# Halving the columns of each matmul in the second product of a feed-forward

## Chip, cores and metric

The kernel runs on one core of one Trainium2 chip. The metric is the device time in microseconds from start to end of one execution; lower is better. The core's engines are TensorE (PE, with its weight loads shown apart as PEld), VectorE (DVE), ScalarE (ACT), GpSimd (POOL) and SyncE (SP), whose queue issues the DMAs.

## What is computed

Attention with two sparse masks, and a feed-forward with an exact Gelu on its result. There are 8 sequences of 576 tokens with 8 heads of 64 channels. Half the heads look at a band of 32 keys, half at every 32nd key. Cut to what matters:

```python
scores = np.matmul(q, k.transpose(0, 1, 3, 2)) / np.sqrt(D)
mask_local   = (rel >= 0) & (rel < 32)
mask_strided = (rel >= 0) & (pos[None, :] % 32 == pos[:, None] % 32)
attn = softmax(np.where(masks, scores, -1e9))     # first 4 heads local, last 4 strided
x = np.matmul(attn, v)                            # -> [4608 tokens, 512 channels]
h = x @ w_in                                      # [512, 2048]
g = 0.5 * h * (1.0 + erf(h / sqrt(2)))
out = g @ w_out                                   # [2048, 512], float32
```

## The kernel before

The 4608 tokens are cut into 12 tiles of 384, and the 2048 hidden channels into 16 chunks of 128. One step of the feed-forward is one chunk of one tile, so there are 192 steps.

Matrix products are made in a rounded float32 format (float32r) in two parts, a high part and a low part that holds the rest. Each product is three matmuls: high by high, high by low, low by high. A step n has three pieces:

- `ffn_h` (lines 541 to 543), the first product: the step's weights `w1` are stationary and the tokens `x` move, 384 columns a matmul. Four channel chunks by three parts are 12 matmuls into one PSUM bank `H`, of which there are two.
- `ffn_g`: ScalarE applies Gelu in PSUM (line 550) and rounds to the high part `gh` (552); VectorE makes the low part `gl` (554).
- `ffn_o` (lines 580 to 582), the second product: blocks of 128 tokens of `gh` or `gl` are stationary, and the 512 output channels of `w2` move. Three blocks by three parts are 9 matmuls a step. Each block has its own PSUM bank `O`, which collects all 16 chunks of a tile; `start` is set on the first matmul of a tile and clears the bank for accumulation.

After the last chunk of a tile `store` copies each bank to `ob` on ScalarE (line 587), and SP writes it to the output (589).

The local heads run on TensorE in 36 jobs (`local_job`: scores at line 251, transposes at 257, products with v at 266). The strided heads run on VectorE (lines 416 and 458), except those of the first tile, which go through TensorE. The weights arrive as 64-bit words and are split into their two float32r parts in `split_w` (lines 144 to 166) on ScalarE and VectorE at the start.

The order of work is set in two ways. Up to step 15 the list `START` gives the order on each engine by hand. From step 16 on the loop over `step(n)` issues `ffn_h(n)`, `ffn_g(n)` and `ffn_o(n - 2)`. There only ScalarE's order is fixed (`manual_schedule(engines={ET.Activation})`), and a planner with costs and due times of its own orders the other engines. The last call issues the second product of the last two steps together, a block of tokens after another.

Of the kernel before, what the change touches and what calls it, by code (L numbers as in the profile page):

```python
# [10 lines left out]
F32 = mybir.dt.float32  # L11
# [12 lines left out]
P = 128  # L24
STRIDE = 32          # band width and stride of the two masks
TT = 384             # tokens of an FFN tile
LU = 64              # queries of a unit of the local heads
LK = LU + STRIDE     # its keys
TR = TT // STRIDE    # its rows of 32 tokens
NGR = 16             # groups of strided heads that the tensor engine takes  # L30
MA = TT // NGR       # tokens of a group
NEG = -8.0e9         # -1e9 before the scale of 1/8
UR = 4               # rows of a unit of the strided heads

# The order of work: (sequence, first row, end row). The strided heads of the first NA tiles go
# through the tensor engine.
NA = 1
# [3 lines left out]
# The start, up to FFN step NB, in the order of each engine's instructions: a word is the next part  # L41
# of a piece of work. Loads: q and k (q) and v (v) of a local job, q and k (S) and v (B) of the strided
# heads of a tile, q and k (E) and v (e) of the first other strided heads, a chunk of weights (w).
# Pieces: local jobs (L), strided heads of a tile on the tensor engine (halves a and b, then A) and
# in units (u), splits of a chunk of weights (c), FFN steps (f).
NB = 16
# [13 lines left out]
# The chunks of weights whose first, second and fifth steps are on VectorE, ScalarE and ScalarE  # L60
# [4 lines left out]
QUOT_V = (0, 2, 3, 4)   # local jobs of the start whose quotients are on VectorE  # L65
# [3 lines left out]
def units(most):  # L69
    """(visit, sequence, first row, rows, tile, its row there): rows of one visit and one tile."""  # L70
    res = []
    for k, (vi, b, r) in enumerate(ROWS):
        if res and res[-1][0] == vi and k % TR and res[-1][3] < most:
            res[-1][3] += 1
        else:
            res.append([vi, b, r, 1, k // TR, k % TR])
    return res
# [7 lines left out]
def attn_ffn_kernel(ctx: ExitStack, tc: tile.TileContext, qk, vl, qka, va, qs, ks, vs, w, out):  # L85
# [6 lines left out]
    NF = w.shape[0]              # hidden chunks  # L92
    NC = DM // P                 # channel chunks
# [4 lines left out]
    JPT = NJ // NTILE            # jobs of a tile  # L98
# [18 lines left out]
    mask = const.tile([P, LK], F32, name="mask")      # a band of STRIDE keys for each query  # L117
    mask0 = const.tile([P, LK], F32, name="mask0")    # the same for the first unit of a sequence

# [3 lines left out]
    # ------------------------------------------------------------------ weights  # L123
    wst, w1, w2 = {}, {}, {}

    def slot(name, shape, dtype=F32):
        """8 KiB a partition: resident weights, and before them what the start needs."""
        return wpool.tile(shape, dtype, name=name, tag="w")
# [5 lines left out]
    def split_w(f):  # L134
        """float64 words -> the leading 24 bits in float32, in two float32r parts."""
        raw = wst.pop(f)
        word = raw.bitcast(U32).rearrange("p (n two) -> p n two", two=2)
        high, low = word[:, :, 1], word[:, :, 0]
        half = raw.bitcast(I16).rearrange("p (n e) -> p n e", e=4)
        byte = raw.bitcast(U8).rearrange("p (n e) -> p n e", e=8)[:, :, 3]  # L140
        hf = high.bitcast(F32)
        # low word: the 3 bits below the high word's, and the sign
        if f in LOW_V:
            nc.vector.tensor_scalar(half[:, :, 0].bitcast(U16), half[:, :, 1].bitcast(U16), 13, None,
                                    ALU.logical_shift_right)
        else:
            nc.scalar.activation(half[:, :, 0], byte, AF.Copy, scale=1.0 / 32, bias=-0.49)  # L147
        yield
        if f in SIGN_S:
            nc.scalar.activation(half[:, :, 1].bitcast(F16), hf, AF.Copy, scale=2.0 ** -60)  # L150
        else:
            nc.vector.tensor_scalar(half[:, :, 1].bitcast(U16), half[:, :, 3].bitcast(U16), 0x8000, None,
                                    ALU.bitwise_and)
        yield
        # exponent from a bias of 1023 to one of 127: the high word, read as float32, by 2**-112
        nc.scalar.activation(hf, hf, AF.Copy, scale=2.0 ** -112)  # L156
        yield
        nc.vector.scalar_tensor_tensor(high, high, 3, low, ALU.logical_shift_left, ALU.bitwise_or)
        yield
        wt = slot(f"w_{f}", [P, 2, 2 * DM], F32R)  # L160
        if f in HIGH_S:
            nc.scalar.copy(wt[:, 0, :], hf)  # L162
        else:
            nc.vector.tensor_copy(wt[:, 0, :], hf)
        yield
        nc.vector.tensor_tensor(wt[:, 1, :], hf, wt[:, 0, :].bitcast(F32), ALU.subtract)  # L166
        w1[f] = wt[:, :, 0:DM].rearrange("p t (c f) -> p t c f", c=NC)
        w2[f] = wt[:, :, DM:]

    # ------------------------------------------------------------------ x tiles  # L170
# [7 lines left out]
    # ------------------------------------------------------------------ local heads  # L178
# [25 lines left out]
    def softmax_parts(blocks, nq, scores, msk, p, nmax, ssum, rs, dve):  # L204
        """Four steps over blocks of scores: mask and maximum, exponentials, sums, quotients."""
# [31 lines left out]
    def local_job(x, banks=None, dve=0, pn=-1):  # L237
        """Local heads of two units: blocks (head pair, unit) of two heads' scores, [2 * LU, LK]."""
# [37 lines left out]
    # ------------------------------------------------------------------ strided heads, first tiles  # L276
    ka = {}

    def load_a(t):
        """Group g has the tokens NGR * m + g of tile t."""  # L280
# [16 lines left out]
    def half_tile(t, o, bank):  # L297
        """Strided heads of tile t: attention of half o of the groups, [(head, query), (group, key)]."""
# [41 lines left out]
    def strided_tile(t, banks):  # L340
        """The same, attended values: [(head, query), token, channel], a bank for each row of PE tiles."""
# [23 lines left out]
    # ------------------------------------------------------------------ strided heads  # L365
# [15 lines left out]
    def load_strided(gr, nm):  # L381
        """q, k or v of the visits that share one buffer."""
# [94 lines left out]
    def alternate(us, what, first):  # L477
        """The steps of several units in turn, so that those which build on each other stay apart:
        of a unit the first ones, then a row of queries after another, then the last one."""
# [22 lines left out]
    def unit_job(us):  # L502
        """Several units, in parts of one engine each."""
        n = 8                        # steps of a part
# [26 lines left out]
    # ------------------------------------------------------------------ FFN  # L531
    hps, gs, ops_ = {}, {}, {}
    ready = [t * NF for t in range(NTILE)]       # first step of a tile
    xfree = [0, 0] + ready[1:-1]                 # first step that may write its x
# [22 lines left out]
    def runs(t, a):  # L557
        """Parts of a block of P columns of a tile that are consecutive tokens."""
# [10 lines left out]
    def ffn_o(*ns):  # L569
        """Chunks of hidden channels into the outputs, a block of tokens after another."""  # L570
# [3 lines left out]
        for a in range(TT // P):  # L574
            o = ops_[t][a]
            sl = slice(a * P, (a + 1) * P)
            for n in ns:
                f = n % NF
                gh, gl = gs[n]
                nc.tensor.matmul(o, gh[:, sl], w2[f][:, 0, :], start=(f == 0), stop=False)  # L580
                nc.tensor.matmul(o, gh[:, sl], w2[f][:, 1, :], start=False, stop=False)  # L581
                nc.tensor.matmul(o, gl[:, sl], w2[f][:, 0, :], start=False, stop=(f == NF - 1))  # L582
# [8 lines left out]
    # ------------------------------------------------------------------ plan  # L591
    strided = []                 # (tile, cost, op)
    N0 = 17
    U0 = sum(x[4] <= NA for x in PLACE)      # those of tile NA are in the plan of the start
# [38 lines left out]
    # a query's residue and no later: the difference's sign and lowest bits are zero  # L633
# [7 lines left out]
    # ------------------------------------------------------------------ start  # L641
# [10 lines left out]
    def job(name):  # L652
        """The parts of a piece of the start, one engine each."""
# [36 lines left out]
    active = []                  # [generator, job, stages done]  # L690
# [56 lines left out]
def lay_out(q, k, v, w_in, w_out):  # L747
    """The inputs in the order in which the chip reads them."""
# [4 lines left out]
    # local heads: two units a job, [job, (j d), pr, unit, token] for heads 2 * pr + j  # L753
# [5 lines left out]
    def pick(a, tok):            # [job, unit, token, h, d]  # L759
# [6 lines left out]
    def groups(a):               # [tile, m, g, h, d] of the first tiles  # L766
# [3 lines left out]
    def padded(a):               # to 32 tokens a group  # L770
        return np.concatenate([a, a[:, 0:32 - MA]], axis=1)

    def by_row(a):               # [b, (h r), row, d]
# [36 lines left out]
```

## Time and profile before

| | |
|---|---|
| median of 2 runs | 948.04 us (947.17 to 948.91) |
| span of the profiled execution, first to last instruction | 946.0 us |
| mean granted TensorE clock over the span | 0.981 |
| busy: PE, PEld | 905.5 us, 792.6 us |
| busy: DVE, ACT | 698.1 us, 523.7 us |
| matmuls of the first product | 2304, of 384 columns |
| matmuls of the second product | 1728, of 512 columns |

The profile is of one execution. Its own time as a run isn't listed apart; its span stands 1.2 to 2.9 us under the two runs. Times are from the span's start. A row of a timeline gives the start in microseconds, the duration in microseconds, the engine, the line, the operation, and the tiles as out<-in. A row of a group gives the busy time and the mean duration of one in ns, and behind the second bar the idle time before it with what ended it. Matmuls are pipelined: a record runs from the start to the modelled end, and records of neighbours overlap.

### The profile page before, as it was taken

How to read it: one execution, taken by the hardware profiler on the slowest of the kernel's cores; microseconds unless marked ns; L12 is line 12 of the kernel's file. 1: busy time of each engine (PE TensorE's matmuls, PEld its weight loads, DVE VectorE, ACT ScalarE, POOL GpSimd, SP SyncE). 2: the span in 40 equal slices, each digit the busy share in tenths (PEclk: the TensorE clock that was granted, in tenths of full speed). 3: DMA queues.
4: the chain of work that ended last, by engine and by line, in shares of the span. 5: the costliest groups of instructions: out<-in, count | busy, mean ns of one | idle time of the engine just before them, and what ended most of it. 6: DMA issues, size and time to landing. Idle time of an engine off the chain costs nothing.

```text
span 946.0 us, 17929 instructions
## 1 busy us (share of the span) xinstructions
PE 905.5 (96%) x5588; PEld 792.6 (84%) x5588; DVE 698.1 (74%) x4831; ACT 523.7 (55%) x1113; POOL 8.1 (1%) x56
## 2 busy tenths in 40 slices
PE   4688889999999999999999999999999999999998
PEld 3576678888888888888888888888888888888997
DVE  5677689957999599678968987786999897561110
ACT  6999977545655535536535455445555544542222
POOL 1000000000000000000000000000000000000000
PEclk8599999999999999999999999999999999999999
DMA  9925320201121013002011112011211200100001
GB/s 332 338 80 200 126 82 24 73 23 57 48 73 56 24 48 105 25 23 82 24 58 60 49 29 88 23 49 47 69 32 40 90 24 1 59 1 1 34 1 34
DMA packets 21872, 62.24 MB, mean 66 GB/s; under 512 B 2576, under 2 KB 3856, under 8 KB 19728
## 3 DMA queue, kind: packets, MB, share of 16 engines
q1 hardware_dynamic: 21776, 61.09, 19.4%
q8 instruction: 44, 0.72, 0.3%
q14 instruction: 52, 0.43, 0.1%
HBM read 51.64 MB, written 9.44 MB: 65 GB/s over the span
## 4 chain that ended last, share of the span: by engine, by line
PE 87%; ACT 11%; DMA 1%; issue 1%; DVE 1%; SPq 0%; ACTq 0%
PE H L541 14%; PE H L543 14%; PE O L582 13%; PE O L581 13%; PE H L542 13%; PE O L580 13%; ACT ws L150 3%; ACT ws L147 3%; PE S_L L251 3%; PE X_L L266 2%; ACT ws L156 2%; PE S_L L257 1%; DMA qka<-in_qka_dram 1%; ACT w L162 1%; ACT H L550 1%
## 5 line engine op out<-in xcount | busy, mean ns | idle before, releaser
L541 PE MATMUL H<-xh,w 128*128 128x384 f32 x768 | 266.1, 347 | 0.9 <-ACT w L162 0.9
L543 PE MATMUL H<-xh,w 128*128 128x384 f32 x768 | 262.9, 342 | 1.1 <-DVE w L166 1.0
L550 ACT ACTIVATE H<-H 128x384 f32<-128x384 f32 x192 | 92.5, 482 | 303.0 <-PE H L543 279.4
L542 PE MATMUL H<-xl,w 128*128 128x384 f32 x768 | 260.0, 338 | 0.0
L458 DVE SCALAR_TENSOR_TENSOR acc<-sv,sc,acc 128x64 f32<-128x64 f32 x1158 | 244.3, 276 | 0.6
L580 PE MATMUL O<-w,gh 128*128 128x512 f32 x576 | 226.5, 393 | 12.7 <-ACT gh L552 12.7
L582 PE MATMUL O<-w,gl 128*128 128x512 f32 x576 | 228.4, 399 | 0.1
L581 PE MATMUL O<-w,gh 128*128 128x512 f32 x576 | 228.3, 396 | 0.0
L554 DVE TENSOR_TENSOR gl<-H,gh 128x384 fp32r<-128x384 f32 x192 | 106.0, 552 | 147.5 <-ACT gh L552 147.0
L416 DVE CUSTOM_DVE_ANT_0 junk<-sq,sk 128x64 f32<-128x64 f32 x1290 | 204.9, 216 | 0.1
L541 PEld LDWEIGHTS H<-xh,w 128*128 128x128 f32 x768 | 145.8, 190 | 11.0 <-ACT w L162 1.3
L542 PEld LDWEIGHTS H<-xl,w 128*128 128x128 f32 x768 | 145.8, 190 | 6.0 <-DVE xl L235 0.2
L543 PEld LDWEIGHTS H<-xh,w 128*128 128x128 f32 x768 | 145.5, 189 | 3.9 <-DVE w L166 2.2
L580 PEld LDWEIGHTS O<-w,gh 128*128 128x128 f32 x576 | 108.5, 188 | 32.7 <-ACT gh L552 15.1
L582 PEld LDWEIGHTS O<-w,gl 128*128 128x128 f32 x576 | 108.5, 188 | 25.4 <-DVE gl L554 3.1
L581 PEld LDWEIGHTS O<-w,gh 128*128 128x128 f32 x576 | 108.4, 188 | 18.3
L416 DVE DVE_READ_ACCUMULATOR2_ANT sc<- 128x1 f32 x1290 | 103.2, 80 | 0.0
L552 ACT CAST gh<-H 128x384 fp32r<-128x384 f32 x192 | 92.7, 483 | 5.9
L550 ACT ACT_TABLE_LOAD x38 | 48.8, 1283 | 0.7
L213 ACT ACTIVATE P_L<-P_L,nm_L 128x96 f32<-128x96 f32 x136 | 48.8, 360 | 0.0
L251 PEld LDWEIGHTS S_L<-qk 64*64 64x64 f32 x576 | 27.7, 142 | 22.9 <-issue 13.0
L426 ACT ACT_TABLE_LOAD x35 | 44.9, 1283 | 0.6
(86 smaller groups left out, 611.6 us busy)
## 6 DMA issues: line engine op xcount, KB each, us to landing
ws<-in_w_dram SPq DMA_DIRECT2D x16, 1024.0 KB, 10.1
qk<-in_qk_dram SPq DMA_DIRECT2D x36, 320.0 KB, 3.0
out_dram<-ob SPq DMA_DIRECT2D x34, 256.0 KB, 2.2
vl<-in_vl_dram SPq DMA_DIRECT2D x36, 192.0 KB, 2.7
sk<-in_ks_dram SPq DMA_DIRECT2D x8, 576.0 KB, 4.9
sv<-in_vs_dram SPq DMA_DIRECT2D x8, 576.0 KB, 3.7
sq<-in_qs_dram SPq DMA_DIRECT2D x4, 576.0 KB, 3.9
sq<-in_qs_dram SPq DMA_DIRECT2D x3, 448.0 KB, 3.6
```

The lines of the kernel that those rows point to most:

```text
L251: nc.tensor.matmul(s[rows(j), cs], qv[rows(j), i, :], kv[rows(j), i, :], start=True, stop=True)
L416: nc.vector.tensor_tensor_reduce(junk, sq[vi, "q"][:, r0 + r, :], sq[vi, "k"][:, c, :], 1.0, 0.0, ALU.mult, ALU.add, ss[u][:, r, c:c + 1])
L458: nc.vector.scalar_tensor_tensor(acc[:, r, :], sq[vi, "v"][:, c, :], wgt, acc[:, r, :], ALU.mult, ALU.add)
L541: nc.tensor.matmul(hp, w1[f][:, 0, c, :], xh[:, c, :], start=(c == 0), stop=False)
L542: nc.tensor.matmul(hp, w1[f][:, 0, c, :], xl[:, c, :], start=False, stop=False)
L543: nc.tensor.matmul(hp, w1[f][:, 1, c, :], xh[:, c, :], start=False, stop=(c == NC - 1))
L550: nc.scalar.activation(hp, hp, AF.Gelu)
L552: nc.scalar.copy(gh, hp)
L554: nc.vector.tensor_tensor(gl, hp, gh.bitcast(F32), ALU.subtract)
L580: nc.tensor.matmul(o, gh[:, sl], w2[f][:, 0, :], start=(f == 0), stop=False)
L581: nc.tensor.matmul(o, gh[:, sl], w2[f][:, 1, :], start=False, stop=False)
L582: nc.tensor.matmul(o, gl[:, sl], w2[f][:, 0, :], start=False, stop=(f == NF - 1))
```

## The change

In `ffn_o` each matmul is split into two over halves of the output channels, 256 columns each. For a block of tokens the three matmuls of the first half come first, then the three of the second. `start` is set on the first matmul of the first half alone, and the check on accumulation groups is switched off for these matmuls, since two groups now share a bank. The rest of the diff takes comments and docstrings away and leaves the lines empty, so lines up to 579 keep their numbers.

```diff
             for n in ns:
                 f = n % NF
                 gh, gl = gs[n]
-                nc.tensor.matmul(o, gh[:, sl], w2[f][:, 0, :], start=(f == 0), stop=False)
-                nc.tensor.matmul(o, gh[:, sl], w2[f][:, 1, :], start=False, stop=False)
-                nc.tensor.matmul(o, gl[:, sl], w2[f][:, 0, :], start=False, stop=(f == NF - 1))
+                for i in range(2):
+                    hs = slice(i * (DM // 2), (i + 1) * (DM // 2))
+                    nc.tensor.matmul(o[:, hs], gh[:, sl], w2[f][:, 0, hs], start=(f == 0 and i == 0),
+                                     stop=False, skip_group_check=True)
+                    nc.tensor.matmul(o[:, hs], gh[:, sl], w2[f][:, 1, hs], start=False, stop=False,
+                                     skip_group_check=True)
+                    nc.tensor.matmul(o[:, hs], gl[:, sl], w2[f][:, 0, hs], start=False,
+                                     stop=(f == NF - 1), skip_group_check=True)
```

## Prediction

> **What bounds the kernel now.** I read the profile page first: how busy each engine is, and which work the chain that ended last is made of.
>
> ```profile
> span 946.0 us, 17929 instructions
> PE 905.5 (96%) x5588; PEld 792.6 (84%) x5588; DVE 698.1 (74%) x4831; ACT 523.7 (55%) x1113; POOL 8.1 (1%) x56
> PE 87%; ACT 11%; DMA 1%; issue 1%; DVE 1%; SPq 0%; ACTq 0%
> L580 PE MATMUL O<-w,gh 128*128 128x512 f32 x576 | 226.5, 393 | 12.7 <-ACT gh L552 12.7
> L582 PE MATMUL O<-w,gl 128*128 128x512 f32 x576 | 228.4, 399 | 0.1
> L581 PE MATMUL O<-w,gh 128*128 128x512 f32 x576 | 228.3, 396 | 0.0
> L580 PEld LDWEIGHTS O<-w,gh 128*128 128x128 f32 x576 | 108.5, 188 | 32.7 <-ACT gh L552 15.1
> ```
>
> TensorE (PE) is the bound: 87% of the chain. The change touches three lines, 580 to 582, of 576 matmuls each: 1728 in all, every one with its own load of weights (PEld), also where line 581 follows 580 with the same gh block. So splitting them makes 1728 more matmuls and 1728 more loads; no load is saved by the weights being the same.
>
> Next, where in the span this counts. The windows view gives PE's busy time by stage, and the chain shows where TensorE takes over.
>
> ```profile
> 50.00:100.00 50.00, 40.41 (x190) 31.69 (x185) 34.78 (x116) 49.86 (x52) 0.00 (x0) 0.95 0.34 129
> 150.00:200.00 50.00, 50.00 (x302) 43.44 (x303) 43.23 (x362) 25.02 (x61) 0.40 (x3) 1.00 0.14 43
> 200.00:300.00 100.00, 100.00 (x614) 88.34 (x611) 87.48 (x658) 55.21 (x128) 0.79 (x6) 1.00 0.19 59
> 800.00:900.00 100.00, 100.00 (x566) 89.11 (x565) 41.17 (x174) 39.63 (x92) 0.00 (x0) 1.00 0.07 23
> ...
> 123.03 0.37 ACT gh L552
> 123.45 0.50 PE O L580
> ...
> 0.00:123.40 123.40, 15.75 (x36) 7.04 (x36) 0.86 0.57 206
> 123.40:946.00 822.60, 210.77 (x540) 101.45 (x540) 1.00 0.14 45
> ```
>
> The columns of a window are its length, then busy time and count of PE, PEld, DVE, ACT and POOL, then the granted clock. Until about 123 us the chain runs through ScalarE (the splitting of the weights), and TensorE has gaps. From 150 us on TensorE has none at all, at a granted clock of 1.00. The last two rows are line 580 alone: 36 of its 576 matmuls lie before the chain turns to TensorE, 540 behind. So 540 x 3 = **1620 matmuls** of the second product sit on the path; the other 108 are covered by ScalarE's work before 123 us, and if that cover were gone they would cost the same each.
>
> A matmul's record (393 ns) overlaps with the next one's. What counts is the distance from one start to the next, so I read the timeline, at three places.
>
> ```profile
> 44.04 0.52 PE L543 MATMUL H<-xh,w 128*128 128x384 f32 x1
> 46.60 0.52 PE L542 MATMUL H<-xl,w 128*128 128x384 f32 x1
> ...
> 930.63 0.33 PE L541 MATMUL H<-xh,w 128*128 128x384 f32 x1
> 931.67 0.39 PE L580 MATMUL O<-w,gh 128*128 128x512 f32 x1
> ...
> 938.17 0.39 PE L581 MATMUL O<-w,gh 128*128 128x512 f32 x1
> 941.79 0.39 PE L582 MATMUL O<-w,gl 128*128 128x512 f32 x1
> ...
> 44.00:46.60 2.60, 2.60 (x9) 2.60 (x9) 1.84 (x3) 2.54 (x4) 0.00 (x0) 0.50 1.00 412
> ```
>
> Eight distances lie between the first two rows, at a granted clock of 0.50 (last row): 320 ns for 384 columns. Six lie between the next two: 1.04 us / 6 = 173.3 ns for 384 columns at full clock. Sixteen lie between the last two: 3.62 / 16 = 226.3 ns for 512 columns.
>
> **The change part by part.** (a) *The columns.* They are the same in number, so only what a matmul costs beside its columns can matter. At half clock 384 columns take at most 320 ns, so at full clock at most 160.0; measured is 173.3. Column for column 512 take 213.3; measured is 226.3. Both leave 13.0 to 13.3 ns: **a fixed 13.2 ns for each matmul**, whatever its width. A matmul of 256 columns then takes 106.7 + 13.2 = 119.9 ns, two of them 239.8, against 226.3: +13.5 ns for each matmul split.
>
> The Trainium skill (TensorE: Matmul & The Clock Gate, "Back-to-back issue gap") has a rule for it: N / 2.4 + 2.5 ns at full clock, which is 109 ns for 256 columns. The trace does not agree on the fixed part: the rows above leave 13.2, not 2.5. By the rule the change would cost 1620 x 2.5 = 4 us, an estimate; this is weighed as a rival below.
>
> (b) *What comes on top in a running step.* The distances above are the cleanest in the trace. A whole step of the feed-forward, 12 matmuls of 384 and 9 of 512 columns, is read from ScalarE's Gelu late in the run, where nothing else is on TensorE:
>
> ```profile
> 927.68 0.47 ACT L550 ACTIVATE H<-H 128x384 f32<-128x384 f32 x1 [3.20 <-PE H L543]
> 936.06 0.47 ACT L550 ACTIVATE H<-H 128x384 f32<-128x384 f32 x1 [3.20 <-PE H L543]
> ...
> 600.41 0.33 PE L541 MATMUL H<-xh,w 128*128 128x384 f32 x1
> 602.51 0.39 PE L580 MATMUL O<-w,gh 128*128 128x512 f32 x1
> 603.90 0.39 PE L580 MATMUL O<-w,gh 128*128 128x512 f32 x1
> ```
>
> Two steps are 8.38 us, one is 4190 ns; 12 x 173.3 + 9 x 226.3 = 4116. So 74 ns a step are extra, 3.5 for each of the 21 matmuls. In mid-run (last three rows) the second product shows 1.39 / 6 = 231.7 ns a matmul. I don't know what the 74 ns are. If they go with the number of matmuls (handing instructions to the array), each new one brings 3.5 more; if they go with time or steps, nothing. The two ends are +17.0 and +13.5 ns for each matmul split. I take the upper, because the clean distances at the end of the run are those of matmuls behind which no more follow.
>
> (c) *The added loads.* A load can run under the matmul before it; the question is how short that matmul may be. The rows where a load isn't hidden:
>
> ```profile
> 315.89 0.19 PEld L543 LDWEIGHTS H<-xh,w 128*128 128x128 f32 x1
> 315.89 0.44 PE L543 MATMUL H<-xh,w 128*128 128x384 f32 x1
> 316.00 0.19 PEld L541 LDWEIGHTS H<-xh,w 128*128 128x128 f32 x1
> 316.17 0.34 PE L541 MATMUL H<-xh,w 128*128 128x384 f32 x1
> ```
>
> After a batch of small attention matmuls the load and its matmul start together. The matmul's record is 0.11 us longer than usual (0.44 against 0.33), and the next load begins 0.11 us later. So a load of 128 columns holds its path for about **110 ns**, though its record says 188, and the matmul behind it streams once they have passed. 110 is under 119.9: the load stays hidden, with 10 ns to spare. Lower bound: nothing. Upper bound, by the record: 188 ns for each half. I take nothing, since the row of 110 is the same instruction in the same neighbourhood.
>
> The Trainium skill ("LDWEIGHTS (loading the stationary operand)", same page) gives columns / 1.2, 107 ns for 128. The 110 ns above agree.
>
> (d) *Order and waits.* No wait is added. A half needs the same gh, gl and weights as the whole, and the bank is released after the same last matmul. From step 16 on the order on TensorE, VectorE and the DMA queue is chosen by a planner with costs of its own, so attention batches may slip by a few matmuls; PE has no gap from 150 to 900 us, so I price this at nothing, +-2 us. If a gap opened, the work queued behind it on TensorE would wait with it. ScalarE and VectorE only get more time for their parts (VectorE is 87% busy in the third window above). The end, a copy and the stores behind the last matmul, is unchanged.
>
> **The sum:** 1620 x 17.0 ns = 27.5 us on the span of 946.0. The two runs of 947.17 and 948.91 us lie 1 to 3 us above that span, and this offset stays: 948.0 + 27.5 = **975.5 us**. With 13.5 ns it is 948.0 + 21.9 = 969.9. With the +-2 us of the order its own range is 967 to 979.
>
> **Rivals.** *B, cost by the column.* If the 13 ns are not per matmul but a slower stream, two halves cost as much as the whole. For it: the running means, 2.10 / 12 = 175.0 ns for 384 columns and 231.7 for 512, are nearly in proportion (0.456 and 0.453 ns a column). A line through them has a fixed part of 4.9 ns, so +4.9 x 1620 = 7.9 us at most: 948 to 956. Against it: the half-clock rows, which leave no room for a slower stream. The skill's 2.5 ns would land here too, at 952.
>
> *C, faster.* If a narrower matmul behind a hidden load escapes the fixed cost, halves are cheaper than the whole. The nearest rows are the transposes of the local heads:
>
> ```profile
> 310.23 0.60 PE L257 MATMUL S_L<-ident,P_L 128*96 128x128 f32 x4
> L257 PE MATMUL S_L<-ident,P_L x136: 270/272/422, 23.8 to 849.2; 128*96 128x128 f32 x136
> ```
>
> Four of them span 0.60 us, with 0.27 for the last: 0.33 / 3 = 109 ns from start to start, each with its own load (96 columns). That is only 2 ns above the 106.7 of 256 full-rate columns. At this pace two halves are 218 ns, 13.7 less than 231.7: 1620 x 13.7 = 22 us off, 926 us. It decides from 115.8 ns a half (half of 231.7) downward, and beyond 2% from 110. Against it: these are other operands at half the columns' pace, and the matmuls of this very form show 13 ns twice.
>
> *D, loads no longer covered.* The slack is only 10 ns. If the fixed 13.2 ns come behind the load (the swap of weights) and the 3.5 of a running step with them, a half takes 110 + 13.2 + 3.5 = 126.7 ns: 2 x 126.7 - 231.7 = 21.7 ns each, +35 us, 983. In the worst case the record of 188 ns is real: 2 x 188 - 231.7 = 144 ns, +234 us, 1182. Farther still, at the transposes' 0.85 ns a column, a half is 217 ns: +328 us, 1276. Against both: the load of 110 ns, and the 384-column matmuls, which start every 173 ns today, below 188.
>
> **How the numbers follow.** Forecast 0.58, B 0.17, C 0.05, D 0.20 (0.15 of it around 983). 2% is 19 us, about what a measurement of this kernel can tell from no change. B and the lower edge of the forecast (0.04) lie within it: 0.21. Faster is C: 0.05. Slower is the rest: 0.74. The range is 951 to 988: it takes in most of B and most of the milder D, and leaves out C (0.05), the bad end of D (0.05) and the flat end of B, about 2 in 10 together.
>
> **What would show it.** In the profile after: 1152 records on each of the three lines; starts 120 to 123 ns apart in a running step; a step of 9 split matmuls up from 4.19 to 4.34 us; load records still near 188 ns, starting with the matmul before; no new gaps on PE. Starts of 116 ns mean B, 110 or less C, 127 or more D. PE gaps after 150 us with a named releaser would mean the order changed, and the sum was of the wrong thing.

## The result and the profile after

The changed kernel takes **955.62 us** (955.38 to 955.86), 7.6 us more than before: a ratio of 1.008, 95% interval 1.0063 to 1.0096. The forecast of 975.5 us had the sign right and the size 3.6 times too large (27.5 us against 7.6). The page after, the lines that answer to those of before:

```profile
span 954.1 us, 21367 instructions
PE 914.7 (96%) x7316; PEld 889.8 (93%) x7316; DVE 698.8 (73%) x4831; ACT 523.6 (55%) x1113; POOL 8.0 (1%) x56
PE 87%; ACT 11%; DMA 1%; DVE 1%; issue 1%; SPq 0%; ACTq 0%
L582 PE MATMUL O<-w,gh 128*128 128x256 f32 x1152 | 326.8, 284 | 11.4 <-ACT gh L552 11.3
L586 PE MATMUL O<-w,gl 128*128 128x256 f32 x1152 | 326.5, 284 | 1.0 <-DVE gl L554 0.3
L584 PE MATMUL O<-w,gh 128*128 128x256 f32 x1152 | 325.7, 283 | 0.0
L582 PEld LDWEIGHTS O<-w,gh 128*128 128x128 f32 x1152 | 219.7, 191 | 14.5 <-ACT gh L552 14.2
```

There are 1728 more matmuls and loads, as the count said. TensorE's share of the chain is the same, and no new wait stands beside the three lines. The windows after (same columns as before) show no gap either: PE is busy all the time, and only its loads have risen, from 88 to 98 us in 100.

```profile
200.00:300.00 100.00, 100.00 (x797) 98.07 (x794) 87.06 (x656) 55.13 (x127) 0.65 (x5) 1.00 0.18 57
800.00:900.00 100.00, 100.00 (x762) 98.89 (x761) 44.53 (x195) 43.55 (x105) 0.00 (x0) 1.00 0.07 23
```

So the time lies in the distances between matmuls. The timeline after, late in the run: two Gelus of ScalarE two steps apart, then starts of halves, and last two starts of the timeline before (the second is also in the prediction).

```profile
935.45 0.47 ACT L550 ACTIVATE H<-H 128x384 f32<-128x384 f32 x1 [3.25 <-PE H L543]
943.92 0.47 ACT L550 ACTIVATE H<-H 128x384 f32<-128x384 f32 x1 [3.25 <-PE H L543]
...
939.49 0.28 PE L582 MATMUL O<-w,gh 128*128 128x256 f32 x1
940.31 0.28 PE L584 MATMUL O<-w,gh 128*128 128x256 f32 x1
941.39 0.28 PE L584 MATMUL O<-w,gh 128*128 128x256 f32 x1
```

```profile
929.57 0.33 PE L541 MATMUL H<-xh,w 128*128 128x384 f32 x1
930.63 0.33 PE L541 MATMUL H<-xh,w 128*128 128x384 f32 x1
```

A step is 8.47 / 2 = 4.235 us, where it was 4.19. The first seven halves of a step stand 0.82 / 7 = 117 ns apart, the next nine 1.08 / 9 = 120.0. So 119.9 for a half was right, and yet a step grew by 45 ns only, not by 121 or 153. The last two rows show where I had misread the kernel before: the first six matmuls of the *first* product, which the change doesn't touch, stood 1.06 / 6 = 176.7 ns apart, not 173.3.

I then took all starts of steps in which no attention matmul falls (69 before, 83 after, all behind 150 us). In ns, "settled" being the distance that a long run of one width comes to (226.7 for 512 columns, 173.3 for 384, 120.0 for 256; e1 below measures them):

| part of a step | settled (before, after) | before | after |
|---|---|---|---|
| second product | 9 x 226.7 = 2040, 18 x 120.0 = 2160 | 2081 (+41) | 2147 (-13) |
| first product, 12 matmuls | 2080 | 2106 (+26) | 2087 (+7) |
| together | 4120, 4240 | 4187 (+67) | 4233 (-7) |

The distances follow the same order in every such step, to within 1 ns. Before: 229 233 236 224 231 236 228 233 231 for the second product, then 171 175 177 185 176 182 and from there on 173. After: 117 117 118 119 121 117 117, from there on 120, then 178 174 175 and 173. So the step grew by 120 in settled distances, and the change took away 74 ns of unevenness that the kernel before had paid. 176 steps x 46.7 ns = 8.2 us; measured from the first matmul of step 16 to the last of all, the stage went from 804.3 to 812.2 us, 7.9 more.

### The profile page after: what moved, and what is told of

Its sections match the earlier page's. It is cut to its first block, busy times and chain, and to the rows that moved or that the text cites. A ratio compares the mean times of both kernels' runs of the same rounds, so it can differ in the third digit from the quotient of the medians.

```text
span 954.1 us, 21367 instructions
## 1 busy us (share of the span) xinstructions
PE 914.7 (96%) x7316; PEld 889.8 (93%) x7316; DVE 698.8 (73%) x4831; ACT 523.6 (55%) x1113; POOL 8.0 (1%) x56
## 4 chain that ended last, share of the span: by engine, by line
PE 87%; ACT 11%; DMA 1%; DVE 1%; issue 1%; SPq 0%; ACTq 0%
PE H L541 14%; PE O L586 14%; PE O L584 14%; PE O L582 13%; PE H L542 13%; PE H L543 13%; ACT ws L150 3%; ACT ws L147 3%; PE S_L L251 3%; PE X_L L266 2%; ACT ws L156 2%; PE S_L L257 1%; DMA qka<-in_qka_dram 1%; ACT w L162 1%; ACT H L550 1%
## 5 line engine op out<-in xcount | busy, mean ns | idle before, releaser
L582 PE MATMUL O<-w,gh 128*128 128x256 f32 x1152 | 326.8, 284 | 11.4 <-ACT gh L552 11.3
L586 PE MATMUL O<-w,gl 128*128 128x256 f32 x1152 | 326.5, 284 | 1.0 <-DVE gl L554 0.3
L584 PE MATMUL O<-w,gh 128*128 128x256 f32 x1152 | 325.7, 283 | 0.0
L582 PEld LDWEIGHTS O<-w,gh 128*128 128x128 f32 x1152 | 219.7, 191 | 14.5 <-ACT gh L552 14.2
L586 PEld LDWEIGHTS O<-w,gl 128*128 128x128 f32 x1152 | 220.3, 191 | 2.9 <-DVE gl L554 2.8
L584 PEld LDWEIGHTS O<-w,gh 128*128 128x128 f32 x1152 | 219.9, 191 | 0.0
L259 ACT COPY PT_L<-S_L 96x512 f32<-96x512 f32 x34 | 19.8, 583 | 44.0 <-PE S_L L257 44.0
```

The source lines that it names most:

```text
L582: nc.tensor.matmul(o[:, hs], gh[:, sl], w2[f][:, 0, hs], start=(f == 0 and i == 0), stop=False, skip_group_check=True)
L584: nc.tensor.matmul(o[:, hs], gh[:, sl], w2[f][:, 1, hs], start=False, stop=False, skip_group_check=True)
L586: nc.tensor.matmul(o[:, hs], gl[:, sl], w2[f][:, 0, hs], start=False, stop=(f == NF - 1), skip_group_check=True)
```

## Experiments

The question: where do the 67 ns a step come from, and why does the change lose them? Theory 1: TensorE itself makes them after each change of width. Theory 2: ScalarE and VectorE make them. Theory 3: they go with the number of matmuls, as the prediction took it.

**e1, widths alone.** A kernel of its own; its core is

```diff
+    for i in range(48):
+        nc.tensor.matmul(junk[:, 0:320], w1[:, i % 2, i % 4, :], w2[:, i % 2, 0:320], start=False, stop=False, ...)
+    ...                      # the same for 512, 384, 256, 192, 128
+    for k in range(6):       # part A; B with halves, C with two steps at a time
+        h(hb)                # 12 of 384
+        o(ga[0], ga[1], k == 0)
```

> A kernel of its own: it leaves the attention and nearly all of the feed-forward out and only runs matmuls of the kernel's form (its output isn't the reference's). First 48 matmuls in a row of each width, 512, 384, 320, 256, 192 and 128 columns, every one with its own load of 128 columns. If a matmul costs its columns plus a fixed 13.3 ns, the starts settle at 226.7, 173.3, 146.7 and 120.0 ns for the first four; if the cost goes by the column (0.452 ns, rival B) at 231, 173, 145 and 116. For 192 and 128 columns the fixed cost gives 93.3 and 66.7, unless a load holds its path for 110 ns: then both stand at 110 to 114. Then steps on TensorE alone: part A 12 of 384 and 9 of 512, part B 12 of 384 and 18 of 256, part C 24 of 384 and 18 of 512. Theory 1: a change of width is followed by some 8 to 15 matmuls at uneven distances, and this is made by TensorE itself; part A then takes 4187 ns a step like the kernel before (67 over the settled 4120), part B 4233 like the kernel after (7 under the settled 4240), and part C 4150 a step, since its changes are half as many. Theory 2: the extra comes from ScalarE and VectorE, which read and write PSUM at that time; parts A to C then take 4120, 4240 and 4120, and only part D, which has the Gelu and the two splits, takes 4187 with 512 columns and 4233 with 256. Theory 3: it comes with the number of matmuls handed to TensorE: A and C both 4187, B above 4240.

Its timeline: runs of 48 of one width (320, 256, 192, 128), then the start of the next part.

```profile
29.35 7.19 PE L53 MATMUL J<-w,w 128*128 128x320 f32 x48
36.38 5.92 PE L55 MATMUL J<-w,w 128*128 128x256 f32 x48
42.13 5.50 PE L57 MATMUL J<-w,w 128*128 128x192 f32 x48
47.47 5.50 PE L59 MATMUL J<-w,w 128*128 128x128 f32 x48
52.80 0.39 PE L63 MATMUL Ha<-xh,w 128*128 128x384 f32 x1
```

From start to start: 7.03 / 48 = 146.5 ns for 320 columns, 119.8 for 256, then 111.3 for 192 and 111.0 for 128. With 226.7 and 173.3 from the runs before them, four widths lie on one line: 26.7 ns for 64 columns and **13.3 ns for each matmul**. Rival B's cost by the column is out. At 192 and 128 columns the distance no longer follows the columns: the loads of 128 columns set it, at 111 ns. Where the line (2.4 columns a ns, and 13.3) meets these 111 ns is an estimate, some 235 columns; no run has a width between 192 and 256. That 111 ns are not merely the price of handing over a matmul with its load, the kernel before shows: from 315.27 to 315.89 us it starts 16 small matmuls of line 266, each with a load of 64 columns, 39 ns apart on average.

Part A, TensorE alone, no other engine at work:

```profile
54.94 0.39 PE L73 MATMUL O<-w,gah 128*128 128x512 f32 x1
57.02 0.33 PE L63 MATMUL Ha<-xh,w 128*128 128x384 f32 x1
58.09 0.33 PE L63 MATMUL Ha<-xh,w 128*128 128x384 f32 x1
59.13 0.39 PE L73 MATMUL O<-w,gah 128*128 128x512 f32 x1
```

Nine of 512 take 2.08 us, the first six of 384 1.07, the other six 1.04: 4.19 a step, with the same order of distances as in the kernel. Part B gives 4233 a step and part C 8307 for two, 4153 a step. These are theory 1's numbers for all three (4187, 4233, 4150); VectorE, ScalarE and GpSimd do nothing in these parts, so theory 2 falls, and with C below A so does theory 3. Part D, with Gelu and splits, shows the same distances again.

**e2 and e3, half as many changes in the real kernel.** The second product of two steps is issued together, on the kernel before and on the changed one:

```diff
-gpool = ... bufs=3          +gpool = ... bufs=4        # and the output's buffers 3 -> 2
-        elif n >= NB + 2 and n < NS:
-            ffn_o(n - 2)
+        elif n >= NB + 2 and n < NS and n % 2:
+            ffn_o(n - 3)
+            ffn_o(n - 2)
```

> The kernel before, but from step 16 on the second product of two steps is issued together every second step: 24 matmuls of 384 columns, then 18 of 512, with half the changes of width (the Gelu's buffers are 4 instead of 3, the output's 2 instead of 3). Theory 1 (uneven distances after a change of width, 67 ns a step): half of it goes, 34 ns a step over some 175 steps, 6 us: 942. Theories 2 and 3 (other engines, number of matmuls): nothing goes, 948.

> The same pairing on the changed kernel: 24 of 384, then 36 of 256. Theory 1: its uneven distances are 7 ns a step below the settled ones, half of that is lost, 175 x 3.5 ns = 0.6 us: 956 where the changed kernel had 955.6, so the halves now cost 14 us against the paired kernel with 512 columns, twice the 7.6 us of the change. Theories 2 and 3: no difference from the changed kernel, and still 7.6 us against the paired one with 512.

e2 takes 943.74 us against 948.5 on the same chip, ratio 0.9955 (0.9938 to 0.9973); e3 956.6, ratio 1.0087 (1.0072 to 1.0102). e2 moved as theory 1 said, by somewhat less (942 was forecast, 948 by the other theories). The time of e3 can't tell theory 1's 0.6 us from nothing, but its clean steps (no attention matmul in them) can: two take 8473 ns, 3.4 ns a step more than in the changed kernel, where theory 1 said 3.5. The halves now cost 12.9 us where they had cost 7.6, though nothing about the halves is different: what they had hidden was the other kernel's unevenness. The timeline of e2, a pair's 18 matmuls of 512:

```profile
423.77 0.39 PE L580 MATMUL O<-w,gh 128*128 128x512 f32 x1
425.85 0.39 PE L580 MATMUL O<-w,gh 128*128 128x512 f32 x1
427.89 0.33 PE L541 MATMUL H<-xh,w 128*128 128x384 f32 x1
```

The first nine take 2.08 us, as ever; the second nine 2.04, settled.

**e4, the cut at another column.**

```diff
-                    hs = slice(i * (DM // 2), (i + 1) * (DM // 2))
+                    hs = slice(0, 384) if i == 0 else slice(384, DM)
```

> The changed kernel with the cut at column 384 instead of 256: as many matmuls and loads, the same columns, but every second matmul is only 128 columns wide. Theory of the load's path (a load of 128 columns holds it for 108 ns and starts 3 ns behind the matmul before, so no matmul starts less than 111 ns after another): a pair costs 173.3 + 111.5 = 285 ns, 45 more than two halves, so 1620 x 45 = 73 us above the changed kernel: 1029. Rival, a fixed 13.3 ns for each matmul and loads that are always covered: 173.3 + 66.7 = 240 ns as with the halves, 956. Rival by the column: 948 to 956.

1035.01 us, ratio 1.0922 (1.0907 to 1.0937), 6 above the forecast of the load's path and far from both rivals. Its timeline, the second and third of 128 columns of a block and the next of 384:

```profile
862.00 0.27 PE L584 MATMUL O<-w,gh 128*128 128x128 f32 x1
862.11 0.27 PE L586 MATMUL O<-w,gl 128*128 128x128 f32 x1
862.22 0.40 PE L582 MATMUL O<-w,gh 128*128 128x384 f32 x1
```

0.11 us apart, as in e1: the loads set the pace. Not one by one, as was expected: in a clean step the second of the three starts 60 ns behind the first, and the first of 384 behind them holds the next for 227 to 233 instead of 173. In all a clean step takes 4700 ns, where the changed kernel has 4233. With as many matmuls and the same columns, the place of the cut alone is worth 79 us.

**e5, twice as many changes.** The kernel before with 6 of the first product, one block of the second, 6 of the first, two blocks of the second:

```diff
-            ffn_h(n)
+            ffn_h(n, range(0, 2))
+            if n >= NB + 2:
+                ffn_o(n - 2, blocks=range(0, 1))
+            ffn_h(n, range(2, NC))
...
-            ffn_o(n - 2)
+            ffn_o(n - 2, blocks=range(1, 3))
```

> The kernel before with twice as many changes of width from step 16 on: 6 matmuls of 384, 3 of 512, 6 of 384, 6 of 512 a step (the same matmuls and as many). Theory 1 (uneven distances after each change): by the measured patterns 18 + 26 + 29 + 26 = 99 ns a step over the settled distances where the kernel before has 67, so 175 x 32 ns = 5.6 us more: 954. The rival, that the 67 ns are paid once a step whatever the order: 948.

956.23 us, ratio 1.0089 (1.0075 to 1.0103): near theory 1's 954, but for another reason. A clean step of its timeline:

```profile
863.09 0.39 PE L580 MATMUL O<-w,gh 128*128 128x512 f32 x1
863.79 0.33 PE L541 MATMUL H<-xh,w 128*128 128x384 f32 x1
864.85 0.39 PE L580 MATMUL O<-w,gh 128*128 128x512 f32 x1
866.24 0.33 PE L541 MATMUL H<-xh,w 128*128 128x384 f32 x1
867.28 0.39 PE L580 MATMUL O<-w,gh 128*128 128x512 f32 x1
```

0.70 + 1.06 + 1.39 + 1.04 = 4.19 us. The 27 clean steps have a mean of 4193 ns, 73 over the settled distances and not 99: the six narrow matmuls pay 20 ns after three wide ones and 4 after six, not 26 each time. So twice as many changes cost 7 ns a step, 1.2 us in all. The other 7.2 of the 8.3 us by which the stage from step 16 on is longer lie in steps with attention matmuls, which the planner set elsewhere; the kind of matmul (first product, second, attention) changes 877 times, against 479. So the 956 came near the forecast by luck, and theory 1's sum failed: the cost of a change depends on how long the run before it was, and e6 shows the same without attention.

**e6, what counts as a change.** Runs of one width after another; same weights, same bank, nothing else at work:

```diff
+    def run(n, w):
+        for i in range(n):
+            nc.tensor.matmul(junk[:, 0:w], w1[:, i % 2, i % 4, :], w2[:, i % 2, 0:w], start=False, stop=False, ...)
+    for w in (480, 448, 384, 320, 256):     # part A
+        run(24, w)
+        run(24, 512)
+    ...
```

> A kernel of its own that leaves the attention and the feed-forward out (its output isn't the reference's): runs of matmuls, all with the same weights, the same bank and no other engine at work. Part A goes from 512 columns to 480, 448, 384, 320, 256 and back, part B from 384 to 320 and 256 and back, 24 of each. If only a change of width does it, every return to 512 costs some 41 ns over the settled 226.7 in its first 9 matmuls, and each step down up to 26 ns; if it needs another product (other weights, another bank), these runs settle at once. Part C has runs of 1, 3, 6, 12 and 15 of 512 between 12 of 384: a run of k should cost 2, 18, 29, 41, 41 ns over the settled time. Part D has runs of 1, 3 and 6 of 384 between 18 of 512. Part E leaves a gap on TensorE before a run of 512: if the uneven distances come from the change of pace and not from the width, they follow a gap as well, some 41 ns; if from the width alone, the run settles at once.

The weights are the same four blocks of one tile in turn in all runs but for the first matmul of part E. Distances between starts in the trace, in ns, up to where they settle:

```
384 -> 512: 229 233 236 224 231 236 228 233 230 | 227 227 226
320 -> 512:     231 236 228 233 231             | 226 227 227
256 -> 512: 233 236 228 233 231                 | 226 227 227
448 -> 512: 230 231 236 228 233 231             | 226 227 227
480 -> 512:                                       226 227 226
512 -> 480: 214 221 212 221 212 221 ...           for all 24
512 -> 448: 200 206 203 202 203 199 207 202 ...   for all 24
512 -> 384: 171 175 177 185 176 182             | 173 173 174
gap -> 512: 341 240 235 233 236 224 231 236 228 233 231 | 226 227 227
```

No other weights and no other bank are needed, so it isn't the second product that is at fault. Coming from other widths the run enters one and the same sequence at a later place, which I had not expected. The expectation for part C held: runs of 1, 3, 6, 12 and 15 of 512 cost 2, 19, 30, 41 and 41 over the settled time. That of part A held for the return from 384 (40); those from 320, 256 and 448 cost 25 to 29, that from 480 nothing. The steps down to 480 and 448 cost more than the 26 expected, 81 and 65 over 24 matmuls, since these widths don't settle in them. Behind a run of 1, 3, 6 or 12 of 512 the 12 of 384 pay 11, 21, 4 or 26. In part D a run of 18 of 512 pays 30, 37 or 41 behind 1, 3 or 6 of 384. In part E a gap does the same without any change of width:

```profile
197.59 0.50 PE L75 MATMUL J<-w,late 128*128 128x512 f32 x1 [2.33 <-ACT late L74]
197.93 4.30 PE L50 MATMUL J<-w,w 128*128 128x512 f32 x18
```

The 2.33 us of waiting are followed by the long sequence. In e1's first run the sequence follows distances of 427 ns, those of half clock: 343 235 234 236 224 231 235 229 232 231 from 12.45 us on (this trace's record of the granted clock begins at 12.68 us, with full clock). So I call it a change of pace: a change of width, a gap or a step of the clock can start it, though not every change of width does (480 to 512). What in TensorE makes the sequence stays open: the runs show when it comes and what it costs, not why.

**e7, control, and e8.** e2 had other sizes of buffers. e7 is the kernel before with these sizes alone; e8 has the pairing with the sizes of before:

```diff
             ffn_h(n)
+            if n >= NB + 2 and n % 2:
+                ffn_o(n - 3)
+                ffn_o(n - 2)
             for _ in ffn_g(n):
                 pass
```

> The control for the paired kernel: the kernel before with its two sizes of buffers (4 for the Gelu's parts, 2 for the output) and no pairing. If the 4.8 us that pairing gained come from fewer changes of pace, this stays at 948, with the same uneven distances (2081 ns for 9 matmuls of 512 columns, 2106 for 12 of 384). If they come from the buffers, it shows 944.

> The kernel before with the second product of two steps issued together every second step, now with its own buffers: the paired products are issued ahead of the step's Gelu, so that the third buffer is free in time. By the control the other sizes of buffers cost 3 to 4 us and hid as much of the paired kernel's gain. Theory 1 (half of the changes of pace, 34 ns a step over 176 steps): 6 us less than before, 942, and if the whole difference to the control counts, 7 to 8 us, 940. Rival (the later Gelu opens gaps on TensorE, or the planner scatters the attention's matmuls more): 946 or above, with idle time of TensorE behind line 552 after 150 us, or more than the 341 changes between the kinds of matmul that the paired kernel had.

e7 takes 952.23 us, ratio 1.0038 (1.0026 to 1.005), neither of the two values expected: the buffers gain nothing, they cost 4 us. ScalarE now waits for the output's buffers (its wait for stores was not among the longest before):

```profile
ACT ob L587 <- DMA out_dram<-ob: 19.4, 11, 2.6
```

and step 16 begins 1.3 us later, the stage behind it is 3.1 us longer. That this wait makes the stage longer isn't shown: TensorE has no gap after 150 us, and a clean step takes 4187 ns as before. The 3.1 us lie in the steps with attention matmuls, which stand in another order (495 changes of kind). e8 takes 943.5 us, ratio 0.996 (0.9946 to 0.9974), 1.5 above the 942 of theory 1. TensorE has no gap after 150 us, but the planner split some pairs: 424 changes of kind, not 341. So a part of the rival was true, and the place of the attention is worth a few us in each of these kernels. e2 and e8 are both below the kernel before and the changed one.

**Clean steps and the rest.** The stage from step 16 on, less 176 clean steps, leaves what the attention's matmuls add: their own time and the uneven distances behind them. e8 isn't in the table, since few of its pairs are whole.

| kernel | a clean step, ns | stage, us | stage less 176 clean steps, us |
|---|---|---|---|
| before | 4186.6 | 804.3 | 67.5 |
| after | 4233.3 | 812.2 | 67.2 |
| e2 | 4153.2 | 800.2 | 69.3 |
| e3 | 4236.7 | 813.3 | 67.6 |
| e5 | 4193.2 | 812.6 | 74.7 |
| e7 | 4186.7 | 807.5 | 70.6 |

In the clean steps e2 gains the 5.9 us that theory 1 asks for, and gives 1.8 back around the attention. Between the kernel before and the changed one the last column hardly moves, so the 7.9 us of the change lie in the clean steps.

## Why the prediction was wrong

- **(a), the fixed cost: right.** 13.2 ns was forecast, 13.3 measured on four widths, and settled halves stand 120.0 ns apart (119.9 forecast). The Trainium skill's 2.5 ns (TensorE: Matmul & The Clock Gate, "Back-to-back issue gap") don't hold for these operands; the measurement decides. The 952 us that followed from them are nearer than my forecast by luck.
- **(b), the 74 ns on top of a step: this step failed.** I priced them at +3.5 ns for each new matmul or, at the other end, at no change. I had not allowed for a third case, that the change removes them. They are 41 ns in the nine wide matmuls, which never settle within a step, and 26 ns in the six narrow ones behind them, together 67; the rest of the 74 is rounding in the rows I used. With halves they become -13 and +7. So each split costs 46.7 / 9 = 5.2 ns, not 17.0. The sentence on which I chose the upper end (that the last matmuls are clean because none follow) was a guess; they are clean because more than nine others of their width come before them.
- **(c), the loads: right.** They stay hidden. The path of 110 ns that I read from one place is 111 from start to start in e1 and e4, so the slack of the halves is 9 ns. The Trainium skill's 107 ns (same page, "LDWEIGHTS (loading the stationary operand)") lie 4 ns below that.
- **(d), order and waits: right.** There is no gap and no new wait. The planner did move the attention (450 changes of kind, not 479), at no cost in sum: 67.5 us around it before, 67.2 after.
- **The count, 1620, was 36 too many.** Step 16 begins at 137.49 us before and 137.83 after, so the halves of the first 16 steps cost 0.3 us together; 176 x 9 = 1584 remain.
- **Rival B** had the size (up to +4.9 ns a split) for a wrong reason. Its running means, 175.0 and 231.7, were the uneven distances averaged in; the stream isn't slower by the column. The 955.62 us lie in the range of 951 to 988 only by the part that took B in; the forecast's own range began at 967.

With (b) at its measured value the sum is 948.0 + 0.3 + 8.2 = 956.5 us, 0.9 above the measurement. What makes the uneven distances inside TensorE stays open.

## What to carry to other kernels

Read the distance from start to start in the order in which the matmuls come, not as a mean: a mean over a short run mixes what a matmul costs with what the change of pace before it costs, and a change that lengthens the run alters both. Keep matmuls of one width together where the order is free; here two steps at a time gained 4 us without any change of work. Before cutting a matmul, compare what is left of its columns with the time of its weight load: 256 columns were just above it, 128 below, and the cut at the other column cost over eleven times as much (87 us against 7.6).

## What the runs showed of the hardware that I had not expected

After a change of pace, matmuls of 512 columns in the kernel take nine distances of 224 to 236 ns before they settle at 226.7, those of 384 six of 171 to 185 before 173.3, those of 256 seven of 117 to 121 before 120.0. Behind other widths or shorter runs (e6) the sequence is shorter. Matmuls of 480 and 448 columns didn't settle in 24: those of 480 alternated between 212 and 221, a mean of 216.7 where 213.3 would be on the line, and those of 448 have a mean of 202.7 where 200.0 would be. With no other engine at work the sequences are the same as in the full kernel.

At half clock the 13.3 ns don't show, only the columns. In the kernel before, at a granted clock of 0.50 (60.7 to 64.0 us), 512 columns take 427 ns, and 384 take 320 (44.0 to 46.6 us); in the changed kernel 256 take 213 (60.8 to 64.1 us, also 0.50). Two halves then cost as much as the whole, so the price of the cut is one of full clock alone.
